# Another table of order and engine for the first 1,000 operations of an attention and Mish kernel

## The chip, the core and the metric

The kernel runs on one core of one Trainium2 chip. The metric is the device time of one execution in microseconds (us); lower is better. Before the change three runs gave 820.86, 822.78 and 823.05 us, so the median is 822.78 us. TensorE is called PE here, VectorE DVE, ScalarE ACT, GpSimd POOL, and SP is the engine that only issues DMAs.

## What is computed

Attention with a mask made of hashes, and a feed-forward layer on its output:

```python
q_bits = (einsum('bhsd,dk->bhsk', q, proj) > 0);  k_bits = the same of k      # proj is 64 x 6
mask = bucket(q_bits)[:, :, :, None] == bucket(k_bits)[:, :, None, :]
scores = where(mask, q @ k.T / sqrt(64), -1e9)                   # 4 batches x 8 heads x 768 x 768
attn = exp(scores - max(scores)); attn = attn / (sum(attn) + 1e-9)
x = (attn @ v) brought to (3072, 512)
h = x @ w_in;  g = h * tanh(softplus(h));  out = g @ w_out       # w_in 512 x 2048, w_out 2048 x 512
```

## The kernel before

The rows of x are cut into 12 units of 256 rows (`u`, three to a batch). Each unit has eight score tiles and eight groups of feed-forward columns. The work comes as 2,978 operations, each a small Python function that emits a few instructions of one engine:

- `S n` (att_front, L894): the score tile n on PE, 128 queries of two heads against 768 keys, into the PSUM tile ps_s (for tiles 1, 3, 5 and 7 into a second one, ps_s2). Behind it the chain `max` (DVE, L906), `scl` (three or four tiny instructions, L912 to L918), `exp` twice on ACT (L932) into the buffers pb, `sums` and `rv` (tiny), `hi` (L387 or L388) and `lo` (DVE, L403) into hl, and a DMA that transposes hl into PT. In the first unit `tp32` on PE and `tc32` on ACT (L978) transpose pb through the score tile's own PSUM instead, so that the next tile but one waits for them.
- `V p` (att_pv, L1015, in the first unit L1022): PE, probabilities times v for a pair of heads; its result becomes X by `x_hi` (ACT) and `x_lo` (DVE).
- `H m` (ffn_h, L1075 to L1077, in the first unit L1071) and `O m s` (ffn_out, L1132 to L1134, in the first unit L1128): the two products of the feed-forward layer, between them `mish` (ACT, L1099) with `g_hi` and `g_lo`.
- Preparation, mostly in the first 160 us: `w_u`, `w_sign`, `w_low`, `w_join` (L555 to L575, and L385 to L388) turn a piece of 64-bit weights into 32-bit floats; `square` (ACT, L437), `st` (two tiny matmuls on PE, L469 and L470), `half` (DVE, L473) and `pw` find a power of two as a scale; `w_hi`, `w_lo`, `v_hi`, `v_lo`, `k_hi` and so on (L387, L388, L403) split values in two 16-bit parts; `hp`, `hsum`, `bits` make the hash. `fill` operations are empty matmuls (L901, L1081).

`exp` and `mish` need different tables on ACT; where one follows the other, an ACT_TABLE_LOAD stands between them.

Nothing is planned at run time. The string ORDER lists the 2,978 numbers, each with a letter when another engine or form than the first is taken: 470c is operation 470 in its third form. `ordered` walks the list, asserts that all predecessors are done, and emits:

```python
for w in ORDER.split():
    n, a = (int(w[:-1]), "abcd".index(w[-1])) if w[-1].isalpha() else (int(w), 0)
    ...
    yield o.alts[a][2]
```

Each engine then works through its own instructions in the order of the list, and waits for others by semaphores. Half of the PSUM tile ps_t is used in turn by `st`, `hp` and every second `V`; the next of them waits until DVE has read the last one (`half`, `hsum`, `x_lo`).

Of the kernel before, what the change touches and what calls it, by code (L numbers as in the profile page):

```python
# [87 lines left out]
164b 3 14 22 1 2 4 88 0 276b 37 167 257b 330 142 23 24 7 6 13 990b 8 66 5 65 63 67 15 17 16 25 38c 40 250 275b 305  # L88
110b 9 10 11b 12 18 348 41 19 42 62 108 43 306b 73 20 21 53c 39c 26b 28 55 64 44 45 74 46 47 29 48 78 30 27c 75 49 76
56 50 77b 79 31 32 89c 349 350 33 34 91 105 70 71 72 83 143b 51 35 206b 80 273b 52 36 81 92 84 85 86 118 104 90c 87  # L90
106 82 168c 93 238 112 94 95 96 141 119 480b 291 128b 54b 107 113 129b 97 99 98 1409b 111 100 114b 120c 160b 101b 222b
203b 183 303b 57 102 157b 58 60 169 253b 292 274b 293 117 252b 158b 489b 611b 310b 351 121 103 184 59 69 116 134c 239
220b 144 137 138 159 204b 170 240 241b 242b 251 139 230 61 145 146b 177 178b 149 148 185 231 122 171 205b 161 154 155
179b 135 186 162 123 140 109b 232 150c 333 68 156 163c 124 151 152 304b 172 126 125 180 173 207 136 187 165 166 188
294b 174 175 415 153 127 197d 208 200 201 236 198 326 209 130b 199 211 212 217 218 416 190 189c 131 233 243 182 181
283 284b 191 133 132 176 202 295b 213c 214 417 237 224 225 215 192 193 226c 219 254 289 255 256b 216b 235 421 290 595b
400 507 228 229 244b 247 258 285 260 234 401 248 313 314b 418 194 286 288 245 402 261 262c 263 195 403 259 249 287 270
419b 781b 271 272 315 277 352b 508 266c 422 307 278 423 279b 308 267 309 316 281 296 196 282 340b 341 346 300 301 246
268 311 312 265 264 319b 297d 509 323 324 318 302 269 342b 608b 327 325 353 510 317 347 298 320 328 329 221 299 321
404b 331 332 322 368b 413 511b 334 424b 335b 343 336c 337 414 512b 354b 355 362 363 357 369b 345 338 339 370b 356b 364  # L100
358 514b 359 420 223b 476 479 513 946b 366 371 367 344 386 394 374c 478 532 372 387 375 360 361 373 389b 388b 395 425
505 506 396 390 481 376b 210 491 380b 515 381 377 398 391 392 399 426b 427 434 435 378 382 533 534 535 379 446b 428b
429 436b 531 393 488 530 438 430 439 536b 493 539b 490 431 537c 432 468 433 440c 383 441 482 447 469 384 638 483 484b
385 470 448b 472 486 442 487 450b 473 594 494 597 540 443 516 497 492b 471b 538 549 596 444 445 548 541 599 550 280b
551 474 451 452c 498 455b 449 406 453 500b 456 475 552 517 518b 604 499 1132b 457b 501 458 553b 556 554b 365b 545b
680b 520 407 454 558 607 521 559 555 503 557 495 405 585 542 522 560 502 460b 610 523 543 459 586 525 524b 461 587 544
526 588 464b 462b 973b 546 528 589 463 465 466c 467 590c 591 547 397b 609 527 504 584 569 561c 562 592b 624 756b 593
612 757b 408 758b 759b 570 409 563b 564b 571 641 529 565 572 626 642 627 760b 761b 625 762b 763b 764b 765b 766b 767b
768b 769b 770b 771b 772 773b 774b 628 775b 643 573 629 411 410 630 567 633c 631c 566 574 227b 665 676 575 576c 666 577
644 645 412 568 634 632 578 579 580 581 582 668 667 776 601 646 496 669 583 600 670 602 603 671b 674 672b 704 705 673  # L110
647b 648b 605 606 616c 613 693 675 650 706 713 684 694 649 685 635 651 617 618c 620b 695 686 683 737 636 687 637 688
619 622 691c 614 615 640 519b 639 692 657c 652 777b 778b 779b 677 658 689b 715 780 659c 690 678 653 741 740 679 621
714 716 1226b 742 681 661 682 785 751 655 654 743 660c 782 744 663 738 811b 623 717 707 752 696 753 754 718 755 719
787 720b 747b 810 477b 697 708 709 783c 722 784 788c 698 951b 147b 812 700 745b 815 817 711 712 833 746 749c 748 930
# [22 lines left out]
1294 1100 1343 1332 1304 1303 1309b 1318 1279 1353b 1310 1270 1354 1381 1308 1319 1311 1313 1320 1293 1312 1315 1371  # L137
# [57 lines left out]
2801 2701b 2642 2643 2644b 2646 2629 2710 2596 2697 2647 2960b 2635 2703 2630 2702 2628 2712 2715 2659 2562 2648b 2649  # L195
# [1093 lines left out]
```

## Time and profile before

| | before |
|---|---|
| median of 3 runs | 822.78 us (820.86 to 823.05) |
| profiled execution: time, span | 823.38 us, 821.6 us |
| PE busy | 794.0 us, 97% of the span |
| DVE busy, ACT busy, POOL busy | 702.8 us (86%), 663.5 us (81%), 52.4 us (6%) |
| mean granted TensorE clock | 0.998 |

The span is the time from the first to the last instruction of the profiled execution; 1.78 us of that execution's time lie around it. The profiled execution is 0.6 us over the median, so a sum made from its rows stands on 823.38 us.

### The profile page before, as it was taken

What the parts mean: (1) busy time and instruction counts of PE and PEld (TensorE: products, weight loads), DVE (VectorE), ACT (ScalarE), POOL (GpSimd) and SP (SyncE); (2) the same over time, 40 slices, a digit from 0 to 9 for tenths busy, and PEclk for the clock granted to TensorE, in tenths of its full rate; (3) what the DMA queues carried; (4) which work ended last, traced back from release to release, by engine and by line L of the source; (5) the groups of instructions that cost most, each with busy time, mean ns of one, the idle gap of its engine ahead of it and who ended that gap; (6) DMA issues with size and microseconds to landing.
All of it is one profiled execution on the core that took longest, in us unless ns stands there. A gap on an engine that the chain in (4) does not pass through costs nothing.

```text
span 821.6 us, 16785 instructions
## 1 busy us (share of the span) xinstructions
PE 794.0 (97%) x6588; PEld 548.8 (67%) x6588; DVE 702.8 (86%) x1351; ACT 663.5 (81%) x1000; POOL 52.4 (6%) x61
## 2 busy tenths in 40 slices
PE   6889999999999999999999999999999999999998
PEld 5657665676667676677677676676576577577664
DVE  5899999999989897899999888899899889789522
ACT  6899999999888889999788798688698788586312
POOL 3453211100000000000000000000000000000000
PEclk9999999999999999999999999999999999999999
DMA  9997987699899697899989779879979777856500
GB/s 259 276 237 217 242 186 162 149 182 213 173 171 170 139 189 143 148 197 193 200 162 204 151 138 171 165 128 219 171 147 200 136 110 128 142 116 128 112 1 26
DMA packets 400303, 135.58 MB, mean 165 GB/s; under 512 B 370528, under 2 KB 391008, under 8 KB 400224
## 3 DMA queue, kind: packets, MB, share of 16 engines
q1 hardware_dynamic: 400224, 134.52, 81.9%
q8 instruction: 51, 0.84, 0.4%
q14 instruction: 28, 0.23, 0.1%
HBM read 35.65 MB, written 6.29 MB: 51 GB/s over the span
## 4 chain that ended last, share of the span: by engine, by line
PE 74%; DVE 10%; ACT 5%; DMA 4%; issue 4%; SPq 2%; POOL 0%; DVEq 0%; ACTq 0%; POOLq 0%
PE ps_s L894 12%; PE ps_t L1015 9%; PE ps_acc L1075 9%; PE ps_acc L1077 9%; PE ps_acc L1076 9%; PE ps_o L1132 8%; PE ps_o L1134 8%; PE ps_o L1133 8%; DVE svb L906 3%; ACT pb L932 2%; DVE hl L403 2%; DMA PT<-hl 2%; DMA stg<-in_v_dram 1%; SPq L420 1%; PE ps_acc L1071 1%
## 5 line engine op out<-in xcount | busy, mean ns | idle before, releaser
L932 ACT ACTIVATE pb<-ps_s,svb 128x768 f32<-128x768 f32 x192 | 188.4, 985 | 40.4 <-DVE svb L918 32.6
L1075 PE MATMUL ps_acc<-X,wi 128*128 128x256 f16 x704 | 192.0, 273 | 0.3 <-ACT ffb L1099 0.3
L1077 PE MATMUL ps_acc<-X,wi 128*128 128x256 f16 x704 | 192.0, 273 | 0.0
L1076 PE MATMUL ps_acc<-X,wi 128*128 128x256 f16 x704 | 191.9, 273 | 0.0
L906 DVE TENSOR_REDUCE svb<-ps_s 128x2 f32<-128x1536 f32 x96 | 168.3, 1753 | 15.8 <-PE ps_s L894 14.8
L403 DVE SCALAR_TENSOR_TENSOR hl<-pb,svb,hl 128x768 f16<-128x768 f32 x175 | 176.1, 1014 | 2.5 <-ACT hl L387 0.5
L894 PE MATMUL ps_s<-KT,QT 128*128 128x512 f16 (+1 forms) x768 | 141.0, 326 | 4.3 <-DMA QT<-tok 1.8
L1132 PE MATMUL ps_o<-wo,ffb 128*128 128x512 f16 x352 | 133.6, 379 | 0.0
L1134 PE MATMUL ps_o<-wo,ffb 128*128 128x512 f16 x352 | 133.5, 379 | 0.0
L1133 PE MATMUL ps_o<-wo,ffb 128*128 128x512 f16 x352 | 133.5, 379 | 0.0
L894 PEld LDWEIGHTS <-QT 128*128 128x128 f16 x768 | 72.1, 97 | 53.1 <-issue 7.5
L1015 PE MATMUL ps_t<-PT,VT 128*64 128x256 f16 x1584 | 95.6, 275 | 3.5 <-DVE hwo L473 2.0
L1015 PEld LDWEIGHTS <-VT 128*64 128x64 f16 x1584 | 84.4, 111 | 17.5 <-issue 17.5
L1099 ACT ACTIVATE ffb<-ps_acc,smalls 128x512 f32<-128x512 f32 x88 | 59.2, 684 | 43.3 <-PE ps_acc L1077 30.3
L387 ACT ACTIVATE hl<-pb,svb 128x768 f16<-128x768 f32 x78 | 71.7, 929 | 20.9 <-DMA PT<-hl 12.3
L1076 PEld LDWEIGHTS <-wi 128*128 128x128 f16 x704 | 68.8, 98 | 12.9 <-issue 0.6
L1075 PEld LDWEIGHTS <-wi 128*128 128x128 f16 x704 | 68.8, 98 | 12.1 <-issue 1.4
L1077 PEld LDWEIGHTS <-wi 128*128 128x128 f16 x704 | 68.8, 98 | 8.1
L403 DVE SCALAR_TENSOR_TENSOR ffb<-ffb,smalls 128x512 f16<-128x512 f32 x88 | 64.9, 746 | 3.5 <-ACT ffb L387 2.4
L1134 PEld LDWEIGHTS <-ffb 128*128 128x128 f16 x352 | 34.4, 98 | 41.6
L1133 PEld LDWEIGHTS <-ffb 128*128 128x128 f16 x352 | 34.4, 98 | 36.9
L388 DVE TENSOR_SCALAR hl<-pb,svb 128x768 f16<-128x768 f32 x89 | 54.6, 617 | 3.4 <-DMA PT<-hl 2.0
(207 smaller groups left out, 1013.6 us busy)
## 6 DMA issues: line engine op xcount, KB each, us to landing
out_dram<-ffb SPq DMA_DIRECT2D x24, 256.0 KB, 2.8
stg<-in_q_dram SPq DMA_DIRECT2D x10, 512.0 KB, 5.0
stg<-in_k_dram SPq DMA_DIRECT2D x12, 384.0 KB, 4.0
stg<-in_v_dram SPq DMA_DIRECT2D x12, 384.0 KB, 4.1
wo<-in_moe_w_out_dram SPq DMA_DIRECT2D x7, 512.0 KB, 4.4
stg<-in_moe_w_out_dram SPq DMA_DIRECT2D x7, 512.0 KB, 5.0
stg<-in_moe_w_in_dram SPq DMA_DIRECT2D x6, 512.0 KB, 5.2
wi<-in_moe_w_in_dram SPq DMA_DIRECT2D x6, 512.0 KB, 5.1
```

The source lines that it names most:

```text
L387: ACT=lambda: nc.scalar.activation(dst, src, AF.Copy, scale=sc),
L403: return [("DVE", 215 + 1.035 * n, port(lambda: nc.vector.scalar_tensor_tensor(out=dst, in0=src, scalar=sc, in1=hi, op0=ALU.mult, op1=ALU. ...
L894: nc.tensor.matmul(sc[:, hh * S + c0 * P:hh * S + c1 * P], QTb[:, u % 2, sl, qi], KTb[:, j, sl, hh * NCH + c0:hh * NCH + c1].rearrange("p ...
L906: op("max", [("DVE", 1790, lambda: nc.vector.tensor_reduce(out=sv[:, 0], in_=sc.rearrange("p (h e) -> p h e", h=2), axis=AX.X, op=ALU.max, ...
L932: EXP[n, hh] = op("exp", [("ACT", 1075, lambda hh=hh, t=t: nc.scalar.activation(pb[:, t], sc[:, hh * S:(hh + 1) * S], AF.Exp, bias=sv[:, 2 ...
L1015: nc.tensor.matmul(pv[hh * D:(hh + 1) * D, 0:256], vt[:, w, hh * NCH + c], pt[:, hh, a * NCH + c].rearrange("p s t -> p (s t)"), start=(x ...
L1075: nc.tensor.matmul(o, wh, X[:, 0, c], start=(c == 0), stop=False)
L1076: nc.tensor.matmul(o, wh, X[:, 1, c], start=False, stop=False)
L1077: nc.tensor.matmul(o, wl, X[:, 0, c], start=False, stop=(c == NCC - 1))
L1132: nc.tensor.matmul(PS[f"o{s}"], gh, hi[:, e], start=first, stop=False)
L1133: nc.tensor.matmul(PS[f"o{s}"], gh, lo[:, e], start=False, stop=False)
L1134: nc.tensor.matmul(PS[f"o{s}"], gl, hi[:, e], start=False, stop=last)
```

## The change

The source is the same but for the string ORDER. All 2,978 numbers are still there once. The first 1,000 places hold the same 1,000 operations in another order, 145 entries of the list have another letter, and behind place 1,000 some twenty operations move, the last of them at place 2,639. The last of the first 1,000 operations runs at 232 us before. The first line of each table, and one line further back:

```diff
-164b 3 14 22 1 2 4 88 0 276b 37 167 257b 330 142 23 24 7 6 13 990b 8 66 5 65 63 67 15 17 16 25 38c 40 250 275b 305
+14 1 2 167 492 37 88 3 4 5 990 22 13 18 63 67 7 6 0 110b 220b 306b 111 251 23 24 25 38c 40 250 140 203b 158b 19 41 73
...
-2278c 2182 2280 2142 2367 2300 2301 2209 2257 2381 2245 2279 2282 2256 2258 2271 2259 2247 2303 2281 2260 2261 2304
+2278c 2182 2280 2142 2300 2301 2209 2257 2381 2245 2279 2282 2256 2258 2271 2259 2367 2247 2303 2281 2260 2261 2304
```

Three places show what that does to an engine's own order. The first is ACT around the score tiles 4 to 6 of the first unit. L932 are the exps, two to a tile (an x2 stands for both; ps_s_89 is ps_s2), L978 the tc32 copies, L387 with VT a v_hi, L387 with wi or wo a w_u. Before:

```order
L932 ACTIVATE pb,svb<-ps_s,svb 128x768 x2
L932 ACTIVATE pb,svb<-ps_s_89,svb 128x768 x2
L978 COPY PT<-ps_s 128x12x128
L387 ACTIVATE VT<-wo,smalls 128x768
L978 COPY PT<-ps_s_89 128x12x128
L387 ACTIVATE VT<-wo,smalls 128x768
L437 ACTIVATE stg,smalls<-wo 128x1024
L945 ACTIVATE svb<-svb 128x2
L932 ACTIVATE pb,svb<-ps_s,svb 128x768 x2
```

and now:

```order
L978 COPY PT<-ps_s 128x12x128
L932 ACTIVATE pb,svb<-ps_s_89,svb 128x768
L387 ACTIVATE VT<-wo,smalls 128x768
L387 ACTIVATE wi<-wi 128x1024
L932 ACTIVATE pb,svb<-ps_s_89,svb 128x768
L932 ACTIVATE pb,svb<-ps_s,svb 128x768
L945 ACTIVATE svb<-svb 128x2
L932 ACTIVATE pb,svb<-ps_s,svb 128x768
L978 COPY PT<-ps_s_89 128x12x128
```

The two exps of tile 5 are parted by a v_hi and a w_u, and tile 5's tc32 has moved behind the exps of tile 6.

The second place is PE behind score tile 13: the O products there, the `st` of one weight scale, and what follows it. Before:

```order
L1128 MATMUL ps_o_916<-wo,ffb 128x512 x2
L1128 MATMUL ps_o_915<-wo,ffb 128x512 x2
L469 LDWEIGHTS ones
L469 MATMUL ps_t<-smalls,ones 128x2
L470 LDWEIGHTS ones
L470 MATMUL ps_t<-floors,ones 128x2
L1015 LDWEIGHTS VT
L1015 MATMUL ps_t<-PT,VT 64x256
```

and now:

```order
L1128 MATMUL ps_o_904<-wo,ffb 128x512 x2
L469 LDWEIGHTS ones
L469 MATMUL ps_t<-smalls,ones 128x2
L470 LDWEIGHTS ones
L470 MATMUL ps_t<-floors,ones 128x2
L1071 MATMUL ps_acc_903<-X,wi 128x256 x8
L728 LDWEIGHTS QT
L728 MATMUL ps_t<-pj,QT 128x12
```

Behind the `st` V5 stood; now H5 and a hash product stand there, and V5 comes only behind S14, H6 and two O.

The third place is ACT between the exps of tile 13 (the first row of both) and those of tile 14 (the last row). L1099 are mish and the table load ahead of it, L437 squares, L1039 the x_hi. Before:

```order
L932 ACTIVATE pb,svb<-ps_s,svb 128x768 x2
L1039 ACTIVATE X<-ps_t,smalls 128x256 x2
L396 COPY tok_65<-tok_64 128x16x64
L437 ACTIVATE wi,smalls<-wi 128x1024
L568 ACTIVATE wo<-wo 128x512
L437 ACTIVATE wo,smalls<-wo 128x1024
L387 ACTIVATE hl<-pb,svb 128x768
L387 ACTIVATE stg<-stg 128x512
L387 ACTIVATE wo<-wo 128x512
L932 ACTIVATE pb,svb<-ps_s,svb 128x768 x2
```

and now, from the row behind the exps of tile 13:

```order
L1099 ACT_TABLE_LOAD
L1099 ACTIVATE ffb<-ps_acc_902 128x512
L945 ACTIVATE svb<-svb 128x2
L387 ACTIVATE stg<-stg 128x1024
L1039 ACTIVATE X<-ps_t,smalls 128x256
L1099 ACTIVATE ffb<-ps_acc_903 128x512
L437 ACTIVATE wo,smalls<-wo 128x1024
L437 ACTIVATE wi,smalls<-wi 128x1024
L1099 ACTIVATE ffb<-ps_acc_902 128x512
L387 ACTIVATE wi<-wi,smalls 128x1024
L387 ACTIVATE wo<-wo,smalls 128x1024
L932 ACT_TABLE_LOAD
```

Three mish and two table loads now stand between the exps of tiles 13 and 14, where none stood. In the whole program ACT has 111 table loads instead of 108.

## Rows read from the trace of the kernel before

**Rows 1.** Busy time by stretch (us): PE, PEld, DVE, ACT, POOL; clock; DMA share; GB/s.

```profile
20.00:80.00 60.00, 51.76 (x472) 38.35 (x473) 53.78 (x116) 55.32 (x85) 27.18 (x28) 1.00 0.89 240
80.00:160.00 80.00, 75.29 (x452) 49.52 (x451) 77.71 (x121) 75.73 (x114) 17.83 (x18) 0.98 0.86 197
160.00:230.00 70.00, 69.16 (x604) 48.18 (x602) 66.46 (x144) 63.33 (x101) 0.00 (x0) 1.00 0.95 180
```

**Rows 2.** What PE waited for, 20 to 230 us: total, times, longest.

```profile
PE ps_t L1015 <- DVE hwo L473: 2.0, 1, 2.0
PE ps_t L1022 <- DVE smalls L473: 1.6, 1, 1.6
```

**Rows 3.** PE in order of time, tiles 13 and 14: start, us, what [idle before].

```profile
107.25 1.46 PE L894 MATMUL ps_s<-KT,QT 128*128 128x512 f16 x8
...
114.16 2.86 PE L1015 MATMUL ps_t<-PT,VT 128*64 128x256 f16 x36 [1.99 <-DVE hwo L473]
116.95 4.65 PE L1071 MATMUL ps_acc<-X,wi 128*128 128x256 f32 x16
121.44 1.46 PE L894 MATMUL ps_s<-KT,QT 128*128 128x512 f16 x8
122.74 3.62 PE L1071 MATMUL ps_acc<-X,wi 128*128 128x256 f32 x16
```

**Rows 4.** Groups of ACT, 0 to 230 us: count, busy us, mean ns.

```profile
L932 ACT ACTIVATE pb<-ps_s,svb 128x768 f32<-128x768 f32 x54 | 53.1, 988 | 6.1 <-DVE svb L916 2.3 <-DVE svb L918 2.2 <-POOL svb L918 0.9
...
L978 ACT COPY PT<-ps_s 128x1536 f32<-128x1536 f32 x8 | 11.5, 1442 | 0.6 <-PE ps_s L973 0.6
...
L1099 ACT ACT_TABLE_LOAD x8 | 10.3, 1283 | 0.1
...
L437 ACT ACTIVATE wo<-wo 128x1024 bf16<-128x1024 f32 x7 | 7.4, 1058 | 0.1
...
L1099 ACT ACTIVATE ffb<-ps_acc 128x512 f32<-128x512 f32 x8 | 4.6, 592 | 0.0
L387 ACT ACTIVATE wi<-wi,smalls 128x1024 f16<-128x1024 f32 x4 | 4.6, 1139 | 1.2 <-POOL smalls L458 1.2
...
L387 ACT ACTIVATE VT<-wo,smalls 128x768 f16<-128x768 f32 x2 | 1.9, 947 | 0.0
```

**Rows 5.** The group of the max on DVE, 0 to 230 us.

```profile
L906 DVE TENSOR_REDUCE svb<-ps_s 128x2 f32<-128x1536 f32 x27 | 47.3, 1752 | 5.4 <-PE ps_s L894 5.0
```

**Rows 6.** DVE in order of time: two w_join.

```profile
50.44 1.22 DVE L575 SCALAR_TENSOR_TENSOR wi<-wo,wi 128x1024 int32<-128x1024 int32 x1
...
53.16 2.03 DVE L575 SCALAR_TENSOR_TENSOR wo<-stg,wo 128x1024 int32<-128x1024 int32 x1
```

**Rows 7.** POOL at the same time as the second.

```profile
54.21 2.19 POOL L560 TENSOR_SCALAR wo<-wi 128x1024 bf16<-128x1024 int16 x1
```

**Rows 8.** PE in order of time: score tiles 5 and 7, the tp32 pair of tile 6, a fill.

```profile
45.41 1.46 PE L894 MATMUL ps_s<-KT,QT 128*128 128x512 f16 x8
...
55.23 1.46 PE L894 MATMUL ps_s<-KT,QT 128*128 128x512 f16 x8 [0.63 <-ACT PT L978]
...
61.05 1.53 PE L973 MATMUL ps_s<-ffb,pb 128*128 128x128 f32 x12
...
66.58 0.61 PE L901 MATMUL ps_g<-ones 128*128 128x128 bf16 x8
```

**Rows 9.** PE in order of time: the end of an O, an `st`, V34 and V35.

```profile
585.26 0.38 PE L1133 MATMUL ps_o<-wo,ffb 128*128 128x512 f16 x1
585.48 0.38 PE L1134 MATMUL ps_o<-wo,ffb 128*128 128x512 f16 x1
586.70 0.17 PE L469 MATMUL ps_t<-smalls,ones 128*128 128x2 bf16 x1 [0.84 <-ACT tok L437]
...
587.14 2.16 PE L1015 MATMUL ps_t<-PT,VT 128*64 128x256 f16 x36 [0.25 <-DVE smalls L473]
...
591.19 2.16 PE L1015 MATMUL ps_t<-PT,VT 128*64 128x256 f16 x36 [0.44 <-DVE X L1042]
```

More of the change, by code (lines that the diff above doesn't have):

```diff
@@ L93 @@
[L93 to L102, printed above, removed]
@@ new lines @@
+129b 86 185 178 60 101 102 103 87 59 168c 107 275b 144 169c 64 72 116 291 680b 186 187b 170 122 137 138 179 123 305
+221 61 71 348 139 611b 145 134b 171 146 149 148 135 130c 124 125 126 180 304b 136 161 162 188b 150d 151 189c 163 127
+181 182 154 155 131 106 190 156 165 166 507 132 133 142 172 173 274b 197c 207 200 201 208 333 209b 210b 202 292 230
+231b 232 222b 293 349 152 175 174 224 212 211 217 218 294 283c 295 233 350 236 508 153 213b 225 226b 191 198 219 214
+254 176 227b 437b 229 228 284 285c 286 237 255 247 248 192 193 400 256b 303b 509 242 199 510 194 511 215 401 249 234
@@ new lines @@
+277 235 259 287 260 261b 351 262 288 326 195 402 781b 352b 313b 258 263 278 244 279 281 266c 289 403b 404 270 271 282
+196 272 297d 608b 216 300 314 245 315c 340c 316 341 267 243 265 342 290 143b 301 307 206b 264 302 405 308 309b 415 311
+312 319c 318 317 246 268 327 328 329b 346 334 335b 336 298 421 269b 416 320 323 299 324 331 321 332 325 354c 322 362
+347 368c 417 343 337 355 353 369b 514 363 356 512b 339 338 357 413 414 476 364b 370b 358 366 367 418 386c 360 406 371
+513 296 387 419b 478 374b 375b 946b 604b 388 422 394 395 390 376c 396 479 345 344 380b 359 361 372 373 365b 532 381
@@ new lines @@
+423 600 382c 505 506 377 515 420 389 481 398 399 391 491 426 446b 493 533 383 392 427 434 435 488 378 379 440b 384 393
+436b 424b 428b 429b 430 447 432 385 534 530 490 438 439 468c 441 442c 443 594 469 470c 482 472 535 450b 536b 537b 448b
+595b 431 407 445 473 433 483 484b 147b 531 541 548 539 486 487 540 471 550 257b 451 516 497 538 549 425 498 569 444
+517 500 551 552 452 499b 518 553 501 453 474 554b 556b 449 503 555 521 520 596 522c 557 523 597 408 494 455b 542 607
+489b 495 598b 599 454 586 585 456 457 543 409 544b 609 587 475 502 584 588 410 589 504 756b 525b 757b 758b 759b 625
@@ new lines @@
+760b 761b 762b 763b 558 764b 765b 766b 767b 768b 458 524c 526 460c 590b 592b 546 591 411 547 570 593 528 461b 559 561c
+459 464b 626 562 462 563b 527 412 627 564 560 571 572 574 565 575 610 769b 770b 771b 772 773b 628 774b 775b 463 465
+567 629 466c 576 467 776 777b 601 577 529 624 665 612 566 602 630b 280 330b 578 496 603b 580 579 605 606 641 568 642
+631 633 643 632 616c 667 1132b 613 635 634 617 582 666 618b 620b 581 614 668 714 583 636 669 644 619 670 637b 751 615
+683 639 645 646 647 671 622 672c 621 640 477b 657 673 648b 674b 658 650 675 737 778b 779b 649 659 684 693 677 676 704
@@ new lines @@
+678 651 713 623 694 660 685 695 679 661 686 681 687 682 705 785 688 652 707 780 691c 689c 692 662 690 973b 715 811 741
+740 663 653 716 696b 787 742 708 697 743 664 698 655 717 753 744 654 793b 754 709 755 718 815 699 782 810 788b 783b
+745c 700 701 820 712 711 790 747c 719 702 784 720b 752 748 746 749c 729 789 730 833 865 951 656 812 738 834 817 722
+703 731 723 706 838 791 750c 796 792 866 733 794 724 795 835 825c 732c 813c 735 814 725 826 721 115b 727 836 837 827
+797 839 829 840 573b 925 798 799 800 801b 734 828c 841 736 930 868 818b 857 726 831 803 932 823b 858 869 830 860 875
@@ new lines @@
+876 310b 164b 1409b 927 867 874 728 804 933c 824 859c 928c 870 945 545 821 935 861 872 873 842 832 880c 802 843 878b
+844 877 805 889 863 819 929 806 808 934 862 881 807 888 968 924 845 890 882 883 891b 884 893 894 916c 846 847 886
+1226b 848c 917 864 950 809 939 850 918 480b 920 940 941 969 985 984 849 638b 947 948c 949 952 953b 885 887 851 895 852
+1007 986 944 943 897 960c 919c 922 921 739 923 954 822 970 961 879 853 854 855 971 972 1021 962 964 974 975 976c 955
+896 1008 963c 966 937 1022b 936 977 1009 519b 956 898 957 1010 485b 978 987 1038 899 965 1046 988 989 980 991 992 1048
@@ L124 @@
+1039 979c 900 397b 1041 982 958c 1013b 901 902c 911 912 1024 1014 904 1049c 1050 1023 981 967 913 905 1043 1044b 1057
+1045 914 1241 1059 1060b 1016 993 1025 1026b 1028 983 1061 1260b 1015c 1079 1095 856 1078 1094 1017 1029 1103 1030b
 1031 1032 959 903c 994 915 1096 906 1018 1019 1020 907 908 1083b 1631 1034 1035 938 1042b 1033 1051 1040 1052 1551b
```

58 lines of the change are left out of this document (18 added, 40 removed).

## The prediction

> **What bounds the kernel now.** I read the busy times by stretch first, to see where the engine with the most work stands idle. PE is the one: 794.0 of 821.6 us. From 160 us it is busy 69.16 of 70 us [rows 1], and the whole run has only 27 us of idle PE, so whatever happens behind 160 us can give back almost nothing, and what is delayed there is paid in full only if PE has to stop. The loss sits ahead of that: PE is idle for 8.24 of the 60 us from 20 to 80, where DVE is busy 53.78 and ACT 55.32, and for 4.71 of the 80 us behind them, where DVE (77.71) and ACT (75.73) are nearly full [rows 1]. So two limits hold there in turn: ACT and DVE with the preparation of weights, and the chains that lead from a score tile to the next one.
>
> Then the waits of PE. The two longest single ones are both for a `half` on DVE, ahead of a V: 1.6 and 2.0 us [rows 2]. In order of time the second stands at 114.16, ahead of V5, and it has a tail: V5 then takes 2.86 us where such a V takes 2.16 [rows 9], and the H6 behind it 4.65 where the H7 after that takes 3.62 [rows 3]. The granted clock of this stretch is 0.98 and that of its neighbours 1.00 [rows 1]: some 2% of 80 us ran at the lower of the two levels, 1.2 instead of 2.4 GHz, after PE had stood idle. The tail is 0.70 + 1.03 = 1.73 us. The Trainium skill ("TensorE: Matmul & The Clock Gate", section "What's actually happening") states that the array's clock is halved when PE has been little busy; the trace agrees, by the 2.86 against 2.16 behind that gap.
>
> I therefore keep one account: PE's **lateness**, the start of a score tile now less its start before, less the PE work that the new order has put ahead of that tile (plus what it has put behind). Total PE work is unchanged, and from 227 us on the order on PE is the same but for four neighbours, so the lateness there is the change of the end.
>
> **The change part by part.** Durations are rows of before; starts come from stepping through the new order by hand, each operation at the later of its engine's release and its inputs. Over the first 1,000 places ACT gives up 7.4 us of work net and takes three table loads of 1.28 more, 3.85 [rows 4]; DVE takes on 3.0 us net, POOL gives up 1.8.
>
> *Up to tile 5.* DVE now has a w_u and a w_sign ahead of the max of tile 1 that POOL or ACT did, each near the 1.22 of a w_join of the same shape [rows 6], and the casts around them are exchanged. Tile 1 comes about 1.9 us later, and the chain of exps and tc32 behind it hands 1.5 on to tile 5 (46.9 after 45.41 [rows 8]), with 0.9 of PE work moved behind it. Lateness **+2.4**. It is the least sure term, because nearly every row there has another neighbour; I bound it by 0 (the chain hides all of it) and +4 (both operations and the moved work in full).
>
> *Tile 5 to tile 7, on ACT.* The exps of tile 5 are now parted by a v_hi and a w_u, and its tc32, for which tile 7 waits, stands behind the exps of tile 6. From 46.9: the tile 1.46, hand-over 0.5, max 1.75 [rows 5], the scl about 0.9, so 51.5. Then on ACT exp 0.99, v_hi 0.95, w_u 1.14 (a w_hi of that size), exp 0.99, two exps 1.98, tc32 1.44 [rows 4], 7.5 in all, and 0.4 for the small ones: 59.4, which is 12.5 behind tile 5, where it was 9.8 (55.23 [rows 8]), thus +2.7. But PE has 3.0 of work more to fill it, among it the tp32 pair of tile 6, 1.53, and a fill, 0.61 [rows 8]. Net **−0.3**. Bounds: −1.5 (tile 6's max is early, the exps do not wait) and +2.7 (the work doesn't fit in the hole).
>
> *V2.* It waited 1.6 for a `half` [rows 2]. Now the V stands behind tile 8, and the weight scale it waits for is long done. What remains between tiles 7 and 13 are waits of 0.1 to 0.2 us that sum to 0.45. Net **−1.15**; bounds −1.6 and 0.
>
> *V5 and the clock.* The `st` stays behind tile 13, yet not V5 but H5 and a hash product follow, then tile 14, H6 and two O. V5 needs the half of ps_t that `half` has read, and `half` has now some 9 us in place of none: the wait of 1.99 and the tail of 1.73 go, −3.7. It is bought on ACT: between the exps of tiles 13 and 14 stand two table loads 2.57, three mish 1.78, two squares 2.12, two w_hi 2.28 [rows 4], a w_u 1.14, an x_hi about 0.5 and the exps of 14, 1.98, together 12.4. From 114.1 that gives 126.7 with 0.2 of waiting for H6; PE is through with V5 at 126.2, and what comes next needs the exps: +0.5. Up to tile 19 smaller waits of both orders cancel to −0.75. Net **−3.95**; bounds −5 and 0, the latter if another stop of PE brings the lower clock again.
>
> *Tiles 19 to 24.* ACT has here a second table load pair that PE's order does not cover: between the exps of tiles 19 and 20 two loads and two mish, 2.57 + 1.2 [rows 4], with two splits of 0.9 each and an ob, put the exps of 20 at 179, one us after PE has nothing else; three smaller waits of 0.3 to 0.6 follow. **+2.4**; bounds 0.5 and 3. From 204 us on PE does not stop, so it is kept.
>
> *The late move.* The O that ran ahead of an `st` at 586.70 now stands behind it. The O is six matmuls that start 0.22 apart (585.26, 585.48 [rows 9]), 1.3 us. The `st` waits for a square whose load came just before, so it does not move; the O fills nothing, and V34 (which waited 0.25 for `half`) starts 1.3 − 0.25 = 1.05 later. V35's wait of 0.44 takes part of that [rows 9]: **+0.6**; bounds 0 and 1.05.
>
> The steps give 2.4 − 0.3 − 1.15 − 3.95 + 2.4 + 0.6 = 0.0.
>
> *What stepping leaves out.* Hand-overs between engines and meetings of DVE with POOL are not in the durations. One such meeting can be read: a w_join took 2.03 beside a w_sign of POOL that took 2.19 [rows 7], and 1.22 without it, 0.81 more [rows 6]. By the Trainium skill ("SBUF — State Buffer", section "Who interferes with whom") the two share a port pair under an exclusive lock and the loser blocks for a whole instruction; by that rule one meeting could cost up to 2.19, two of them would bring the sum to about 827.8, and here 0.81 was measured. I take one meeting more, 0.8, and 1.3 for hand-overs, since the smaller single waits of PE between 20 and 230 us in the order of before are 0.2 to 1.1 us each and a new order has its own: **+2.1**; bounds 0 and 5.
>
> The sum stands on the profiled execution: 823.38 + 0.0 + 2.1 = **825.5 us**, 2.7 over the median of 822.78.
>
> **The rivals.**
> - *The start gets shorter (ends on the other side).* Of the 8.24 us in which PE is idle from 20 to 80 us [rows 1] at least 60%, 5 us, vanish, because ACT is rid of two w_low and several squares there, and my +2.4 and −0.3 were an artefact of stepping. For it: ACT's net −7.4, and DVE's max waits 5.0 of its 5.4 for PE [rows 5], so DVE has room. Against: tile 5's parted exps. With −5 in place of those two and the other steps as they are: −5 − 1.15 − 3.95 + 2.4 + 0.6 + 2.1 = −5.0, so 818.4; with half the V5 term lost, 820.5. Middle 819.5. It decides against me once tile 7 starts before 56 us.
> - *An exchange: the lost waits are replaced one for one.* Lateness within ±1.5 at tile 24, hand-overs hidden: 821 to 824, middle 823. For it: the sum of steps is nil; against: nothing in the trace says the allowance is nothing.
> - *DVE becomes the bound.* Its 3.0 us more, up to 6 of it ahead of the maxes of tiles 7, 11 and 12, land where it is busy 77.71 of 80 [rows 1]. If they are paid in full in the place of the allowance, or if PE stops at exps 14 long enough for the lower clock (another 1.7, as behind V5), the time is 828 to 832, middle 829.5.
>
> **How the numbers follow.** A measurement of this kernel can tell about 0.3% from no change, 2.5 us: below 820.3 is faster, above 825.2 slower. My forecast, 824 to 828, has a chance of 0.42, of which 0.11 lies under 825.2; the exchange 0.25; the shorter start 0.22; DVE 0.11. Faster 0.22, same 0.25 + 0.11 = 0.36, slower 0.31 + 0.11 = 0.42. The range takes the middle of the shorter start and most of DVE's: 819.5 to 830, leaving out a little under 2 in 10. The forecast's own range is 824 to 828.
>
> **What the profile after would show.** Tile 5 near 46.9 and tile 7 near 59.4, with ACT in the exps and tc32 between; PE idle of about 9 us from 20 to 80. No wait of PE for `half` ahead of V2 or V5, H6 at 3.6, and a clock of 1.00 from 80 to 160. PE waiting 0.5 to 1 for ACT ahead of the work on tiles 14 and 20. PE's `st` near 586 waits some 2 us in place of 0.84. It is wrong if tile 7 comes before 56 or after 62, if DVE's maxes and not ACT end PE's waits in the first 130 us, or if the clock still falls.

## The result, and the profile after

The changed kernel took 826.41 us (median of four runs, 826.29 to 826.72) against 822.1 us (820.86 to 823.05, one run more than in the table ahead) before, a ratio of 1.0057 with an interval of 1.0038 to 1.0076: slower, by 4.3 us between the medians. The profiled execution has a span of 824.7 us, 3.1 more than before; it is less than the 4.3 because the profiled execution before was 1.3 us over its median and this one 0.3. The forecast was 825.5, in a range of 819.5 to 830.

Busy time by stretch in the changed kernel (columns as in [rows 1]):

```profile
0.00:20.00 20.00, 13.60 (x138) 11.56 (x139) 10.65 (x39) 14.84 (x22) 9.98 (x18) 0.83 1.01 289
20.00:80.00 60.00, 50.75 (x469) 36.07 (x467) 59.00 (x126) 51.59 (x82) 27.22 (x22) 1.00 0.87 239
80.00:160.00 80.00, 75.15 (x445) 49.16 (x444) 78.98 (x130) 75.18 (x116) 22.87 (x19) 1.00 0.85 187
160.00:230.00 70.00, 68.39 (x606) 47.69 (x604) 66.58 (x136) 63.71 (x103) 0.00 (x0) 1.00 0.91 177
```

The reader is to see two things. The clock from 80 to 160 us is 1.00 where it was 0.98: the fall behind V5 is gone, as forecast. And DVE, which was busy 53.78 of the 60 us from 20 to 80, is now busy 59.00: it has become full where ACT, with 55.32 before, has got room (51.59).

PE in order of time around tiles 13 to 15 (answers to [rows 3]):

```profile
109.97 3.70 PE L1071 MATMUL ps_acc<-X,wi 128*128 128x256 f32 x16
...
116.07 1.47 PE L894 MATMUL ps_s<-KT,QT 128*128 128x512 f16 x8
117.78 3.72 PE L1071 MATMUL ps_acc<-X,wi 128*128 128x256 f32 x16 [0.24 <-ACT ffb L1099]
122.75 0.18 PE L469 MATMUL ps_t<-smalls,ones 128*128 128x2 bf16 x1 [1.25 <-DVE hsum L732]
...
126.42 2.15 PE L1015 MATMUL ps_t<-PT,VT 128*64 128x256 f16 x36
129.16 1.46 PE L894 MATMUL ps_s<-KT,QT 128*128 128x512 f16 x8 [0.58 <-ACT pb L932]
...
136.18 1.46 PE L894 MATMUL ps_s<-KT,QT 128*128 128x512 f16 x8 [1.17 <-ACT pb L932]
```

H5 fills the hole behind the `st`, V5 takes 2.15 us and H6 3.72, and tile 14 starts at 116.07. But the next `st` waits 1.25, and tiles 15 and 16 wait 0.58 and 1.17 us for exps.

The account of lateness, step by step, from the starts of the score tiles in both traces less the PE work that the new order has ahead of each (at tile 5 for example 47.25 − 45.41 = 1.84, with 0.70 of work less, so 2.54):

| stretch | forecast | in the two traces | lateness at its end |
|---|---|---|---|
| up to tile 5 | +2.4 | +2.5 | 2.54 |
| tile 5 to 7 | −0.3 | −0.4 | 2.17 |
| tile 7 to 13 (V2) | −1.15 | −0.5 | 1.65 |
| tile 13 to 19 (V5, clock) | −3.95 | −1.4 | 0.29 |
| tile 19 to 24 | +2.4 | +0.2 | 0.48 |
| tile 24 to 27 (227 us) | 0 | +0.8 | 1.26 |
| behind 227 us | +0.6 | +1.85 | 3.11 |
| left out by stepping | +2.1 | in the rows above | |
| sum | +2.1 | +3.1 | |

Two rows are off by more than two us each way, 13 to 19 and 19 to 24, and one by more than one, behind 227 us. These, and the first one, are what the experiments are about.

### The profile page after: what moved, and what is told of

Its sections match the earlier page's. It is cut to its first block, busy times and chain, and to the rows that moved or that the text cites. A ratio compares the mean times of both kernels' runs of the same rounds, so it can differ in the third digit from the quotient of the medians.

```text
span 824.7 us, 16794 instructions
## 1 busy us (share of the span) xinstructions
PE 794.1 (96%) x6588; PEld 546.8 (66%) x6588; DVE 710.5 (86%) x1362; ACT 660.9 (80%) x1000; POOL 60.1 (7%) x59
## 5 line engine op out<-in xcount | busy, mean ns | idle before, releaser
L932 ACT ACTIVATE pb<-ps_s,svb 128x768 f32<-128x768 f32 x192 | 188.5, 985 | 43.0 <-DVE svb L918 36.3
L1099 ACT ACTIVATE ffb<-ps_acc,smalls 128x512 f32<-128x512 f32 x88 | 59.2, 685 | 43.2 <-PE ps_acc L1077 30.3
L387 ACT ACTIVATE hl<-pb,svb 128x768 f16<-128x768 f32 x79 | 72.8, 930 | 23.9 <-DMA PT<-hl 13.9
```

The costliest lines, as they stand in the source:

```text
L387: ACT=lambda: nc.scalar.activation(dst, src, AF.Copy, scale=sc),
L932: EXP[n, hh] = op("exp", [("ACT", 1075, lambda hh=hh, t=t: nc.scalar.activation(pb[:, t], sc[:, hh * S:(hh + 1) * S], AF.Exp, bias=sv[:, 2 ...
```

## Experiments

### First 1,000 places and the rest, each alone

The list has two parts. One kernel takes the first 1,000 places of the changed list and the places behind as before, the other the opposite (written here in short, not as it stands in the files).

```diff
-ORDER = before[:1000] + before[1000:]
+ORDER = after[:1000] + before[1000:]
+ORDER = before[:1000] + after[1000:]
```

> The first 1,000 places of the changed kernel with the places behind them as before. Theory A, from the two traces: tiles 27 to 34 start 1.26 us later than before, and the other 1.8 us of the 3.1 us of span arise behind 330 us, so this kernel is slower than the one before by 1.3 us only (about 823.5 to 824.5, ratio near 1.0015) and tile 49 starts within 0.3 us of tile 27's lateness. Theory B, the prediction's sizes: the first 1,000 places cost 2.5 us or more and the rest 0.6, so this kernel is slower by 2.5 to 3.5 us (ratio 1.003 to 1.004). If the cost of the first part is only visible at the end together with the second one, tile 49 comes 3 us late here too.

> The first 1,000 places of before with the places behind them of the changed kernel. Theory A: tile 27 starts as before (226.9), tile 49 about 1.5 us late, the end 1.5 to 2 us late, so ratio about 1.002. Theory B: only the O moved behind the st costs something, 0.6 us, ratio 1.0007, tile 49 at 402.3. A third possibility: the moves behind the 1,000th place only cost when PE is already late; then nothing shows here up to 580 us, and the st at 586.7 waits about 2.1 us in place of 0.84.

The first part alone: 825.0 us (823.59 to 828.12), ratio 1.0036 (1.0021 to 1.0051), against 822.14 of the kernel before. The rest alone: 824.34 us (821.18 to 826.67), ratio 1.0022 (1.0009 to 1.0036). By the ratios that is 3.0 and 1.8 us, together 4.8, where the whole has 4.7: the parts add, as far as intervals of over 2 us can tell. So theory A is right for the rest (about 1.8, not 0.6) and theory B for the size of the first part (about 3, not 1.3), though the intervals, 0.7 to 3.0 and 1.7 to 4.2 us, leave the other value out only just. The lateness of the first part's profile says only 0.2 us at tile 27 and at the end, but that profiled run, 823.59, is the fastest of its seven. One trace shows one execution. This first part spreads over 4.5 us, and the kernel before over 3.5 (820.65 to 824.18 in 19 runs); the runs with the POOL move below show where the first part's spread arises.

### The engines of one, the places of the other

145 entries of the list changed their letter as well as their place. Two kernels take the new places with the old letters in the first 1,000, and the old places with the new letters.

```diff
-14 1 2 167 492 37 88 3 4 5 990 22 13 18 63 67 7 6 0 110b 220b 306b 111 251 23 24
+14 1 2 167 492b 37 88 3 4 5 990b 22 13 18 63 67 7 6 0 110b 220b 306b 111 251 23 24
...
-164b 3 14 22 1 2 4 88 0 276b 37 167 257b 330 142 23 24 7 6 13 990b 8 66 5 65 63
+164b 3 14 22 1 2 4 88 0 276b 37 167 257b 330b 142 23 24 7 6 13 990 8 66 5 65 63
```

> The new order of all places with the letters (engine and form) of before in the first 1,000. It tells order from engines. Theory A, meetings of DVE and POOL: in the changed kernel the instructions of DVE are together some 5 us longer than the shortest of their form beyond what they were before, and POOL's too; if the new letters bring those meetings, DVE's busy time falls back from 710 towards 703 us here, and the start of tile 14 and the following tiles gets earlier by 1 to 2 us. Theory B: the letters matter little, the places do: DVE stays at 707 or more, and the time stays within 1 us of the changed kernel. Since places and letters were chosen together, a mixed kernel may also be slower than both (830 us or more), which would say that neither part alone carries the difference.

> The order of before in all places with the new letters (engine and form) in the first 1,000. Theory A: the letters alone bring meetings of DVE and POOL, DVE's busy time rises to 707 us or more, POOL's to 57 or more, and PE loses 2 us or more ahead of tile 27. Theory B: no change of the meetings (DVE 704 or less), and the time is set by which work stands between two score tiles' exps on ACT: 823 to 826. A mixed kernel may be slower than both.

873.91 us (ratio 1.0628) and 863.3 us (1.0496): the third possibility that was named, slower than both. PE is busy 183.26 and 184.95 of the first 230 us, where it is 209.23 before and 207.88 after. It says that letters and places fit each other in both tables, and nothing on which of them costs the 3 us: neither theory is decided by it.

### Two DMA issues in the SP queue

In the places behind 1,000 two DMA issues near 375 us changed places with others. This run is the changed kernel (−) with the two put back (+).

```diff
-1500 1503c 1504 1522 1521 1488 ... 1576 1541 1542 1512 1549
+1500 1503c 1504 1521 1488 ... 1457 1522 ... 1512 1510 1576 1541 1542 1549
```

> The changed kernel with two DMA issues of the SP queue back in their old order (the load that was moved ahead of another one, and one transpose of hl that was moved behind the transpose of a later tile, near 375 us). Theory A: the transpose that waits longer holds up the SP queue, the tok transposes behind it come some 4 us later, ACT waits 1.6 us for one at 399.5 us, and PE loses 1.4 us at the st and score tile 49 (tile 48 is 1.9 late, tile 49 3.4); with it back, tile 49 starts about 2.0 us later than before the change in place of 3.4, and the time falls by 1 to 1.5 us. Theory B: the loss there comes from DVE, where a hash sum stands behind the exps' chain and a hi went from ACT to DVE: then nothing changes here, tile 49 stays 3.4 late.

SP in order of time before, and then in the changed kernel (issues of one kind that follow each other stand in one row):

```profile
376.68 4.05 SPq L420 DMA_TRANSPOSE PT<-hl  x2
380.82 0.53 SPq L416 DMA_DIRECT2D stg<-in_v_dram  x1
383.04 4.98 SPq L420 DMA_TRANSPOSE PT<-hl  x2
388.12 1.48 SPq L420 DMA_TRANSPOSE KT<-tok  x1
```

```profile
380.04 1.27 SPq L420 DMA_TRANSPOSE PT<-hl  x1
382.39 0.37 SPq L416 DMA_DIRECT2D stg<-in_v_dram  x1
385.21 6.76 SPq L420 DMA_TRANSPOSE PT<-hl  x3
392.06 1.47 SPq L420 DMA_TRANSPOSE KT<-tok  x1
```

One transpose of hl that stood ahead of a load now stands behind it and behind a transpose of the next pair, three in a row, and the transposes into KT come 3.9 us later (392.06 and 388.12) where PE is up to 1.9 us late (tile 48). What that does, on ACT and then on PE in the changed kernel:

```profile
399.55 0.84 ACT L437 ACTIVATE tok<-stg 128x768 bf16<-128x768 f32 x1 [1.61 <-DMA KT<-tok]
```

```profile
403.70 0.18 PE L469 MATMUL ps_t<-smalls,ones 128*128 128x2 bf16 x1 [0.77 <-DVE hsum L732]
405.62 1.46 PE L894 MATMUL ps_s<-KT,QT 128*128 128x512 f16 x8 [0.38 <-ACT pb L932]
```

With the two issues back, the same places on ACT and on PE:

```profile
400.68 0.84 ACT L437 ACTIVATE tok<-stg 128x768 bf16<-128x768 f32 x1 [0.56 <-DMA KT<-tok]
```

```profile
405.53 0.17 PE L469 MATMUL ps_t<-smalls,ones 128*128 128x2 bf16 x1
406.93 1.46 PE L894 MATMUL ps_s<-KT,QT 128*128 128x512 f16 x8
```

ACT waits 0.56 in place of 1.61, and PE doesn't wait at either place. From tile 48 to 49 the lateness grows by 1.45 us in the changed kernel and by 0.00 here; in the other profiles with the issues moved it grows by 0.6 to 1.5. Theory A holds for the mechanism. The time, 826.25 us (823.45 to 828.0), ratio 1.0049, isn't told from the changed kernel's: the first 45 us spread more than that, and this profile was 2.05 us later at tile 5 than the changed kernel's (lateness 4.59 and 2.54).

### The O ahead of the `st` again

```diff
-2301 2209 2257 2381 ... 2271 2259 2367 2247
+2301 2209 2257 2367 2381 ... 2271 2259 2247
```

> The changed kernel with the O product back ahead of the st at 588 us. The prediction: the move costs 0.6 us, so V34 and V35 start 0.5 to 1 us earlier, and the end comes 0.6 earlier. Rival: PE is 3 us late there, and the st would not wait any more, so that the place of the O matters nothing: no change within 0.15 us in the trace.

826.82 us (825.73 to 829.26). The `st` now waits 0.17 (1.10 in the changed kernel, 0.84 in [rows 9]), V34 0.25 and V35 0.45. From tile 70 to V35 this kernel makes up 0.79 us and the changed kernel, with its O behind, 0.86. The rival is right on the outcome: the place of the O costs nothing. Its reason needs one word more, for the load is late too, only less than PE: the square that waits for it starts at 587.64 in the changed kernel and 589.09 here, 1.9 and 3.4 us later than before (585.71), where PE is 3.3 and 4.2 us late at tile 70. The O fits into what is left of the wait.

### V5 behind H6 in the kernel before

```diff
-520 407 454 558 607 521 559
+520 407 454 607 558 521 559
```

> The kernel before with one swap on PE alone: V5, which waits 2.0 us for a half at 114.16 us, stands behind H6. Theory of the prediction: the wait and the lower clock behind it (1.73 us) cost PE 3.7 us; with H6 in the hole the gap is under 0.3 us, the clock of 80 to 160 us is 1.00, V5 takes 2.15 and H6 3.6 to 3.7, and score tile 14 starts 1.5 to 2.6 us earlier (it then waits for the exps of tile 13 at 118.8). How much of it stays: if PE sets the end alone, 2 to 3 us, ratio 0.997. Rival: ACT and DVE set the pace from 80 to 160 us, so that the next tiles wait for exps instead: tile 19 starts within 0.5 us of 163.8 and the time is the same.

821.66 us (820.29 to 824.05), ratio 0.9997 (0.9983 to 1.001): the same. PE there:

```profile
112.19 3.70 PE L1071 MATMUL ps_acc<-X,wi 128*128 128x256 f32 x16
115.82 2.16 PE L1015 MATMUL ps_t<-PT,VT 128*64 128x256 f16 x36
118.88 1.46 PE L894 MATMUL ps_s<-KT,QT 128*128 128x512 f16 x8 [0.90 <-ACT pb L932]
...
141.71 1.15 PE L894 MATMUL ps_s<-KT,QT 128*128 128x512 f16 x6 [1.78 <-DMA QT<-tok]
...
143.16 3.58 PE L1128 MATMUL ps_o<-wo,ffb 128*128 128x512 f32 x4
```

And the busy time by stretch at that place, and at 144 us:

```profile
110.00:120.00 10.00, 9.10 (x68) 6.53 (x67) 9.96 (x14) 9.88 (x15) 2.67 (x3) 1.00 0.84 178
120.00:126.00 6.00, 6.00 (x26) 4.18 (x24) 5.94 (x12) 6.00 (x10) 0.91 (x1) 1.00 0.48 113
...
144.00:146.00 2.00, 2.00 (x4) 0.67 (x2) 1.93 (x4) 0.95 (x1) 1.15 (x2) 0.50 1.14 213
```

The wait of 1.99 and the slow V5 and H6 of [rows 3] are gone, and tile 14 starts 2.7 us earlier against its own tile 13. By tile 17 nothing is left. DVE is busy 15.90 and ACT 15.88 of the 16 us from 110 to 126, and waits for exps, a square (0.59 us at 133.66) and a DMA take the place of the hole. One thing more took its share in this execution: behind the wait of 1.78 the clock fell again, to 0.50, and four matmuls of an O took 3.58 us where they took 1.96 before. So 1.6 us of the lead went there, the clock from 80 to 160 us is 0.98 as before and not the 1.00 that was expected, and this trace alone doesn't show that ACT and DVE took the whole lead.

The timed runs tell more. Five of the ten runs of this kernel have a mean granted clock of 1.000, so that no such fall can be in them; their median is 821.54 us. Of the 51 runs of the kernel before that stand beside the experiments, 28 have it too, with a median of 821.97; the other 23 have 822.04. So the fall behind V5 is in less than half of the executions of the kernel before, the median time doesn't depend on it, and without a fall on either side the swap is worth 0.4 us, which isn't told from nothing. The 3.7 us were real on PE in the profiled execution and worth nothing that could be measured at the end.

### The same, with the transpose of q that tile 16 waited for

```diff
-461 587 544 526 ... 593 612 757b 408 ... 759b 570 409 ... 629 411 410 ... 645 412
+460b 610 408 523 ... 461 587 544 409 526 410 411 ... 641 529 412
```

> The kernel before with V5 behind H6, as in the run that had the ratio 0.9997, and with the hash of one third of q made earlier: its hp on PE stands behind H7, its hash sum and bits on DVE behind the scl of tile 14, its DMA transpose into QT ahead of the loads that follow. In the run with V5 alone, tile 14 started 2.6 us early, and it was given back at tiles 16 and 17, the largest part in a wait of 1.78 us of tile 16 for that transpose. Theory A: the transposed tok was what took the gain, tile 16 then starts without that wait, tile 19 starts 1.0 to 2.0 us earlier than before, and the time is 820.0 to 821.3, ratio 0.998. Theory B: ACT and DVE are the bound from 80 to 160 us: another wait (exps, or a square ahead of an st) takes its place, tile 19 is within 0.5 us of 163.8 against its own tile 13, and the ratio is 0.9995 to 1.0005.

823.42 us (821.74 to 824.12), ratio 1.0019 (1.001 to 1.0027). (With the hash moved, part of the attention is computed from other hash bits; every instruction is still there.) Tile 16 doesn't wait for the DMA any more and the clock from 80 to 160 us is 1.00. PE waits for squares on ACT instead, 1.41 us at 133.93, 0.80 at 140.17, and then:

```profile
143.90 0.16 PE L469 MATMUL ps_t<-smalls,ones 128*128 128x2 bf16 x1 [1.77 <-ACT wi L437]
```

A lead of 3.0 us at tile 15 is 0.3 at tile 17, here without a fall of the clock. Theory B holds: in this stretch a lead of PE is not kept. Why the kernel is slower than the one before, by some 1.5 us, stays open: its one trace, of an execution of 822.57 us, ends 0.8 us earlier.

### POOL beside DVE, at 116 us

```diff
-586 585 456 457 543 409
+586 585 456 543 409 ... 756b 525b 457 757b
```

> The changed kernel with one w_low of POOL moved behind the next POOL operation, so that it no longer runs at 115.8 to 117.9 us beside a w_lo of DVE that takes 2.30 us there. Theory A, a meeting: the w_lo takes about 1.27 us as its neighbours do, the w_low 1.35 in place of 2.04, DVE's max of tile 14 starts about 1 us earlier, and the st at 122.75 waits 0.3 to 0.5 us less. Theory B: the w_lo's length has nothing to do with POOL: it stays above 2 us.

In the changed kernel a w_lo of DVE takes 2.30 us, while POOL's w_low takes 2.04:

```profile
116.56 2.30 DVE L403 SCALAR_TENSOR_TENSOR wi<-wi,smalls 128x1024 f16<-128x1024 f32 x1
```

```profile
115.81 2.04 POOL L564 TENSOR_SCALAR wi<-stg 128x1024 int16<-128x1024 uint16 x1 [5.34 <-DVE wi L575]
```

With POOL's moved:

```profile
119.24 1.28 DVE L403 SCALAR_TENSOR_TENSOR wi<-wi,smalls 128x1024 f16<-128x1024 f32 x1
```

```profile
124.68 1.34 POOL L564 TENSOR_SCALAR wi<-stg 128x1024 int16<-128x1024 uint16 x1
```

2.30 becomes 1.28 and 2.04 becomes 1.34: the meeting cost 1.0 on one side and 0.7 on the other. PE gained nothing from it (tiles 14 to 19 are 45.03 us apart, 44.98 in the changed kernel); POOL's w_low then ran beside DVE's bits, which took 1.27 in place of 0.20. This one profile (828.14 us) had another thing in it, busy time and clock from 38 us on:

```profile
38.00:40.00 2.00, 0.92 (x6) 0.93 (x7) 2.00 (x5) 1.54 (x4) 0.00 (x0) 0.86 0.52 69
40.00:42.00 2.00, 1.64 (x10) 1.51 (x9) 1.97 (x8) 1.07 (x4) 0.00 (x0) 0.50 0.94 344
42.00:44.00 2.00, 1.67 (x9) 0.90 (x9) 2.00 (x6) 2.00 (x4) 1.68 (x1) 0.50 0.99 300
44.00:46.00 2.00, 2.00 (x8) 1.16 (x7) 0.35 (x4) 2.00 (x6) 2.00 (x3) 0.50 1.42 189
```

The clock is at its lower level, 1.2 GHz, for some 7 us, after PE had waited 2.23 us for the exps of tile 2. Tile 5 then starts 19.73 us behind tile 2, where it is 17.90 to 17.95 in the profiles of this first part without such a fall.

### POOL beside DVE, at 33 us

That wait of 2.2 us at tile 2 stands in the changed kernel too, on PE:

```profile
38.03 1.53 PE L973 MATMUL ps_s<-ffb,pb 128*128 128x128 f32 x12 [2.20 <-ACT pb L932]
...
40.95 0.16 PE L469 MATMUL ps_t<-smalls,ones 128*128 128x1 bf16 x1 [1.37 <-DVE smalls L473]
...
47.25 1.47 PE L894 MATMUL ps_s<-KT,QT 128*128 128x512 f16 x8
...
59.33 1.46 PE L894 MATMUL ps_s<-KT,QT 128*128 128x512 f16 x8
```

and this is DVE, and POOL, ahead of it:

```profile
32.95 1.52 DVE L397 COPY tok<-tok 128x1024 f16<-128x1024 f16 x1
34.39 1.30 DVE L912 TENSOR_SCALAR svb<-svb,smalls 128x2 f32<-128x2 f32 x1
```

```profile
32.84 1.34 POOL L560 TENSOR_SCALAR wi<-wi 128x1024 bf16<-128x1024 int16 x1
34.27 1.40 POOL L564 TENSOR_SCALAR wi<-wi 128x1024 int16<-128x1024 uint16 x1
```

A copy and a tiny scl end at 34.47 and 35.69, 0.29 and 0.02 us behind POOL's two instructions (34.18 and 35.67). The exps of tile 2 wait for the scl:

```profile
35.92 0.99 ACT L932 ACTIVATE pb<-ps_s,svb 128x768 f32<-128x768 f32 x1 [1.60 <-DVE svb L918]
```

In the kernel before POOL makes that scl, and the same exps wait for it:

```profile
33.61 1.23 POOL L918 TENSOR_TENSOR svb<-svb 128x2 f32<-128x2 f32 x1
```

```profile
34.87 0.99 ACT L932 ACTIVATE pb<-ps_s,svb 128x768 f32<-128x768 f32 x1 [0.86 <-POOL svb L918]
```

The kernel of the experiment moves POOL's three operations of that weight ahead of a sums that POOL waits for:

```diff
-161 162 188b 150d 151 189c 163 ... 292 230 231b 232
+161 162 188b 230 231b 232 150d 151 189c 163 ... 292
```

> The changed kernel with one move on POOL alone: the w_u, w_sign and w_low of one weight (31.6 to 35.7 us) stand ahead of the sums that POOL waits 3.2 us for, so that they run from 28.2 to 32.2 us. Theory A: in the changed kernel DVE's copy of tok (1.52 us where others take about 0.4) and the first instruction of the scl of tile 2 (1.30 in place of 0.33) are held until those two POOL instructions end; the exps of tile 2 and PE's wait of 2.2 us at 38.03 come of it. Then here both take under 0.6, PE's wait at tile 2's transposes falls from 2.2 to under 0.6, score tile 5 starts 1.5 to 2 us earlier against its own tile 2, and with the hole the fall of the clock near 39 to 46 us (seen in two of the five profiles with this first part) is gone. The time: 824 to 825.5 if the gain stays, 826.4 if ACT and DVE take it back by tile 17. Theory B: the two lengths have another cause and stay; PE's wait is above 1.8.

> The same move on POOL in the kernel of the first 1,000 new places with the old places behind them (which took 825.0, ratio 1.0036). Theory A: 822.5 to 824, ratio 1.000 to 1.002, tile 27 within 0.5 us of 226.9. Theory B (no effect that stays): ratio 1.003 to 1.004 again.

The lengths on DVE and the start of the operations on POOL in the first of the two:

```profile
37.77 0.42 DVE L397 COPY tok<-tok 128x1024 f16<-128x1024 f16 x1
38.11 0.22 DVE L912 TENSOR_SCALAR svb<-svb,smalls 128x2 f32<-128x2 f32 x1
```

```profile
33.45 1.11 POOL L385 TENSOR_SCALAR wi<-wi 128x1024 f32<-128x1024 f32 x1 [4.48 <-DMA wi<-in_moe_w_in_dram]
```

1.52 becomes 0.42 and 1.30 becomes 0.22: POOL had held DVE for 1.10 + 1.08 = 2.2 us on the chain to the exps of tile 2. Not all of it is new, for the kernel before has a meeting on the same chain: POOL's tiny instruction takes 1.23 us beside a w_join of DVE, and 0.19 at 46.98. From the end of the max of tile 2 to its exps it is 2.96 us in the changed kernel and 1.77 before, 1.2 more. And the remedy failed, in a way that neither theory named: the weight's piece lands only at 33.4, so POOL stood still for 4.48 us, the sums came behind it, and DVE waited 3.37 for them. PE's wait grew to 3.92, and in this profile the clock fell behind it too. 830.85 us (826.91 to 831.9), ratio 1.0104, and with the old rest 826.68 us, ratio 1.0063 (1.005 to 1.0077). So the meeting is shown, and what its absence would gain is not: no kernel was run that is free of it and on time.

What these two show, with the other profiles, is that a delay in the first 46 us is kept but for 0.4 to 2.3 us. The lateness at tile 5 and at tile 27 is 2.5 and 1.3 us in the changed kernel, 2.5 and 0.2 with the old rest, 3.4 and 3.0, 4.6 and 3.4, 5.4 and 4.0 in the three others with nearly the same list, 5.5 and 3.9, and 7.2 and 6.3 with POOL's move. And from tile 13 on all of them have the same distances: tile 13 to 14 9.17 us, 14 to 19 44.9 to 45.0. Most of the spread of this first part is made ahead of tile 5; from tile 5 to 13 the distances differ by another 1.0 us (58.7 to 59.8).

### The exps of tile 5 side by side

```diff
-277 ... 259 ... 781b 352b 313b 258 263 ... 282 ... 272
+277 235 259 258 ... 282 ... 272 313b 352b
```

> The changed kernel with the two exps of tile 5 side by side again, the v_hi and the w_u between them put behind tile 5's tc32. The prediction's step: the parting costs tile 7 some 2.1 us (0.95 + 1.14 on ACT), which PE mostly fills with other work. Then tile 7 starts 10.0 to 10.6 us behind tile 5 in place of 12.1, and tile 13 starts within 0.7 us of where it did against tile 5. Rival: the maxes on DVE, busy 59.0 of 60 us there, end the wait: tile 7 stays 11.5 to 12.1 behind tile 5.

835.11 us in one run. Tile 7 starts 11.98 us behind tile 5: the rival holds, the parting costs tile 7 nothing. ACT now waits 2.04 us for the scl of tile 6 between the exps of 5 and 6:

```profile
57.56 0.99 ACT L932 ACTIVATE pb<-ps_s,svb 128x768 f32<-128x768 f32 x1 [2.04 <-DVE svb L918]
```

The v_hi and the w_u were no obstacle but a filling. Where they stand now they hold DVE's w_sign, and behind it a rv that PE needs:

```profile
62.21 1.49 DVE L555 TENSOR_SCALAR wo<-wi 128x1024 int16<-128x1024 int16 x1 [4.75 <-ACT wi L387]
```

```profile
69.11 0.69 PE L960 MATMUL ps_g<-ffb,svb 128*64 128x128 f32 x4 [4.78 <-DVE svb L954]
```

## Why the prediction was right, and where its steps failed

**Direction and size.** Slower was given 0.42 and the time 825.5; the span grew by 3.1 us where the sum said 2.1, and the medians by 4.3. The sum stood on errors that cancelled, so that the time came as near as it did is in good part luck.

**Up to tile 5 (+2.4; measured +2.5, and 3.4 to 5.4 in other executions).** The size fits, the reason doesn't. I laid it on tile 1, 1.9 us late by a w_u and a w_sign on DVE; tile 1 starts only 0.6 late (25.05 and 24.43). The lateness is nil at tile 3 and arises at tile 4. Ahead of it DVE was held twice by POOL, 2.2 us in all, shown by the lengths with POOL's operations moved; 1.2 of that is new against the kernel before. That is the "meeting" that stood in the allowance with 0.8. That the rest of the lateness hangs on it too, by the `st` that waits 1.37 us for a `half` of the late DVE, is argued from the order in time and not shown. Over the first 230 us the instructions of DVE in the changed kernel are together some 4 us longer beyond the shortest of their line and names than before (22.0 and 18.0 us), and POOL's as well (9.0 and 5.2); DVE's busy time rose by 7.7 us where 3.0 was forecast, and POOL's by 7.7 where 1.8 less was forecast. The Trainium skill ("SBUF — State Buffer", section "Who interferes with whom") says that the loser of the shared ports blocks for the whole instruction. The traces agree: a scl of 0.22 us took 1.30 and ended within 0.02 us of POOL's instruction. I gave that rule less weight than one row of 0.81.

**Tile 5 to 7 (−0.3; −0.4).** Tile 7 at 59.33 against 59.4, yet again by another chain: with the exps joined tile 7 comes at the same distance and ACT waits for the scl of tile 6, so the max and scl on DVE set tile 7, and not the v_hi and w_u on ACT.

**V2 (−1.15; −0.5)** and **V5 and the clock (−3.95; −1.4).** The wait ahead of V2 is gone, but an H now waits 1.00 us for an X of DVE at 75.16, which the sum didn't have. What happens at V5 was right to the tenth: from tile 13 to 14 the lateness falls by 3.71, the clock is 1.00, V5 and H6 run in 2.15 and 3.72 us. The step that failed is the account: it took what PE gains as kept. The kernel before with V5 and the transpose of q moved shows that it isn't: a lead of 3.0 us is 0.3 two tiles later, in waits for ACT and with the clock at 1.00. With V5 alone moved the time stays the same, ACT and DVE being at 99% from 110 to 126 us. In the changed kernel the lead was gone by tile 16. And the tail of 1.73 us was that of one execution; most runs of the kernel before have no fall of the clock at all. (The prediction also reads a mean of 0.98 as 2% of the 80 us at the lower level; with that level at 0.50 it is 4%. The sum took the tail from the lengths and is not touched.)

**Tiles 19 to 24 (+2.4; +0.2).** The exps of tile 20 start at 178.62, as reckoned (179), but PE has work up to 180.33 and waits only 0.40 for them ahead of tile 21; the three smaller waits did not come. This row is 2.2 us too dear and the one ahead of it 2.5 too good: they offset each other by chance.

**The late moves (+0.6; +1.85).** The wrong one was priced. The O costs nothing, since PE is already late there; the `st` near 586 waits 1.10 and not some 2 us. The DMA issue that moved in the SP queue near 375 us, which I had not priced at all, costs up to 1.5 at tile 49. The places behind 1,000 alone measure 1.8 us. What makes the rest of these 1.8 (up to 0.8 us between tiles 27 and 48) was not separated.

**The rivals.** DVE as the bound, given 0.11, describes the stretch from 20 to 80 us best (59.0 of 60 us busy), though its price of 828 to 832 was too high; the 3.0 us that it names give 826.4. The shorter start did not come: PE is idle for 9.25 of those 60 us, 8.24 before.

**The signs of being wrong.** Tile 7 came within its bounds. The clock did fall, though not behind V5 but from 12 to 20 us. And of the 11.8 us that PE waits from 20 to 130 us ACT ends 7.3 by the profile, but the exps that end the longest wait, 2.20, and the one of 0.62 ahead of tile 7 waited themselves for DVE.

What stays open: what makes the 3 us of the first part, of which the meeting at 33 us was seen but not removed; what the falls of the clock add in the timed runs (the one run of the changed kernel with a mean clock of 1.000 took 826.38 us, at the median, so little of it is to be expected there); and what the new table would give without the two meetings. No version that was run beats the kernel before.

## What to carry to other kernels

A hole on one engine is a gain only if the engines that feed it have room behind it: read their busy shares over the same 10 us before you count it, and move that one instruction alone to see if the time follows. In this kernel a delay in the first 46 us was kept for the most part, while a lead of PE at 116 us was not. Before a fall of the clock goes into a sum, see from the clocks of the other runs how many of them have it. When an order changes, list the neighbours across engines that share something, and every queue, DMA issues included: the two costs that the traces show here were a tiny DVE instruction behind a POOL instruction and a transpose behind another one.

## What the runs showed of the hardware

The granted clock fell in the changed kernel in a place where it didn't before: 0.61, 0.50, 0.50 and 0.69 in the four stretches of 2 us from 12 to 20 us, after waits of 0.26 and 0.74 us between short matmuls; score tile 0 took 2.72 us in place of 1.46. In other executions of the same first part the column reads 1.00 there, but tile 0 took 2.77 and the short products were long from the start, so that the clock had not risen yet: up to its first change the column reads 1.00 whichever level holds, and the length of a matmul tells which. Both ways end 0.6 to 1.6 us late at tile 1.

The same wait of PE at tile 2 was followed by a fall of the clock in some executions and not in others: after 2.21, 2.22 and 2.23 us it fell to 0.50, after 2.20, 2.20 and 2.26 it stayed at 1.00.

Order and engine of one table are a pair: mixing the letters of one list with the places of the other costs 41 to 52 us.
